# Zero matrix products among the first four tiles, setup work shared out over three engines, and a later test for the general path, in a biased-attention and channel-mix kernel

## The chip, the cores and the metric

The kernel runs on one core of one Trainium2 chip, as a single launch. The metric is the device time of that core in microseconds (us); lower is better. A core has a matrix engine (PE, with its weight loads PEld), a vector engine (DVE), a scalar engine (ACT), GpSimd (POOL) and a queue engine (SP) that here issues nearly all the transfers. Each engine works through its own list of instructions in a fixed order and waits on semaphores for the others.

## What is computed

The inputs are q, k, v of shape (4 batches, 8 heads, 768 positions, 64) and the weights of a channel mix with 512 model and 1024 hidden channels. Attention is causal within a window of n_local = 96 positions and sees n_global = 8 first positions as well, with a linear distance bias for each head; its output goes through the channel mix.

```python
scores = q @ k.T / 8 - slope[h] * dist          # dist = 96 for global keys outside the window
scores = where(is_global | is_local, scores, -1e9)
a = softmax(scores) ; x = a @ v                  # heads side by side: (4, 768, 512)
xk = mu_k * x + (1 - mu_k) * x_prev              # x_prev: one position earlier, zero at the start
xr = mu_r * x + (1 - mu_r) * x_prev
out = sigmoid(xr @ w_r) * (relu(xk @ w_k) ** 2 @ w_v)
```

The weights arrive as 64-bit floats and are split on the chip into a high and a low part, so that each product of the channel mix is three products on PE (high by high, high by low, low by high).

## The kernel before

**Tiling.** There are 24 tiles of 128 query positions, six to a batch. A loop over 25 steps runs `scores(step, hp)` for the tile of that step in four pairs of heads `hp`, `transposes(step - 1, hp)` for the tile before, and `weighted(step - 2, i)` for the one before that. Scores go to PSUM; DVE adds the bias pattern and takes the row maximum (L312), ACT takes the exponential (L313), DVE forms the reciprocal of the sum (L319, L320), DVE or POOL scales (L323), PE transposes (L335), ACT copies to SBUF (L337), and PE multiplies by v (L354). Two tiles make a chunk, and the channel mix of a chunk (`ffn`, L439) is cut into 40 pieces on PE that `run_ffn` threads between the attention steps from step 3 on; `mix` makes xk and xr (L378 to L383), `channel_mix` makes the products (L393 to L395), and L436 makes the output, which SP stores (L437).

**Weights.** The 20 blocks of 128 by 512 weights are loaded and split during the first steps: `weight_begin` issues the load from SP (L165) into a buffer that is shared with others, takes it through ACT (L172 for the eight blocks of w_k, L175 for the others), POOL (L173, w_k alone), DVE (L176 for the others, then L177, L178, L179) and ACT again (L180), and `weight_end` forms the low part on DVE (L186). `weights_go` after each head pair says how many blocks are to be begun and ended.

**The first microseconds.** SP loads the two sizes (L48) and the tiles of q, k and v. POOL makes the index ramps (L112 to L114) and then clears the upper halves of the two q buffers (L213) and of the three k buffers (L216), since the first eight tiles (`native`) multiply 128 rows of which 64 are zero. DVE turns the ramps and the sizes into distances (L115 to L125, L134 to L137). The bias pattern of a batch's first tile, `pat0`, has eight heads: six are made on DVE (L129), two on POOL (L131). The pattern of all other tiles, `pat`, is made half on ACT (L141) and half on POOL (L143). PE starts with ten products of a zero tile (L93), whose output `idle` nobody reads; they share three PSUM buffers (tag `f`) with the channel mix.

**The general path.** `wide()` handles sizes outside the fast path's limits. Seven small DVE instructions (L609 to L615) turn the sizes into a flag, every engine loads the flag into a register (L617) and branches on it (L618). With the given sizes the branch is not taken.

**What sets the order.** The program text gives each instruction a priority. A scheduler that replays the program on a simulated timeline then picks, for each engine, the ready instruction of highest priority, and that order is fixed in the program that runs. So an instruction need not run where it stands in the text: the flag's seven instructions are the last ones in the text, and the trace has them between 5.89 and 10.1 us. The tiles' buffers are given out by the same scheduler.

Of the kernel before, what the change touches and what calls it, by code (L numbers as in the profile page):

```python
# [9 lines left out]
F32 = mybir.dt.float32  # L10
F32R = mybir.dt.float32r
BF16 = mybir.dt.bfloat16
I32 = mybir.dt.int32
U32 = mybir.dt.uint32
AF = mybir.ActivationFunctionType
ALU = mybir.AluOpType
# [9 lines left out]
GMAX = 8  # L26
BACK = 96
LMAX = BACK + 1
# [11 lines left out]
def tile_biased_attention_channel_mix(ctx: ExitStack, tc: tile.TileContext, qT, kT, v, n_sizes, mu_kr, w_k, w_v, w_r, q_rows, k_rows, v_rows, slopes, out):  # L40
    nc = tc.nc
    vec, act, pool, pe = nc.vector, nc.scalar, nc.gpsimd, nc.tensor

    const = ctx.enter_context(tc.tile_pool(name="const", bufs=1))
# [6 lines left out]
    ngf, nlf = sizes[:, 0:1], sizes[:, 1:2]  # L51
# [34 lines left out]
    ps_f = fast.enter_context(tc.tile_pool(name="ps_f", bufs=3, space=PSUM))  # L86


    zeros = const.tile([128, 512], BF16, name="zeros")
    vec.memset(zeros, 0.0)  # L90
    for i in range(10):
        idle = ps_f.tile([128, 512], F32, name="idle", tag="f")
        pe.matmul(idle, zeros[:, 0:128], zeros, start=True, stop=True)  # L93

# [2 lines left out]
    pat0 = const.tile([128, H, 128], BF16, name="pat0")  # L99
# [4 lines left out]
    def piece():  # L104
        edge.append(next(cut))
        return btmp[:, edge[-2] : edge[-1]]

    ints, flts, local, glo, dist0, dist = (piece() for _ in range(6))
# [16 lines left out]
    vec.scalar_tensor_tensor(dist0, glo, nlf, local[:, 96:224], op0=ALU.max, op1=ALU.min)  # L125
    for h in range(H):
        c = -8.0 * 2.0 ** -(h + 1)
        if h < 6:
            vec.tensor_scalar(pat0[:, h, :], dist0, c, None, op0=ALU.mult)  # L129
        else:  # L130
            pool.tensor_scalar(pat0[:, h, :], dist0, c, 1.0, op0=ALU.mult, op1=ALU.mult)  # L131
# [6 lines left out]
    for h in range(H):  # L138
        c = -8.0 * 2.0 ** -(h + 1)
# [58 lines left out]
    def weights_need(n):  # L198
        weights_go(n, n)
# [5 lines left out]
    state = {}  # L205


    q_zero, k_ring = [], []
    for i in range(3):
        if i < 2:  # L210
            q_zero.append(q_pool.tile([128, H, 128], F32, name=f"qz_{i}", tag="qh"))
            kz = kw_pool.tile([128, H, W], F32, name=f"kz_{i}", tag="kw")[:, :, 0:128]
            pool.memset(q_zero[i][64:128], 0.0)  # L213
        else:
            kz = q_pool.tile([128, H, 128], F32, name=f"kz_{i}", tag="ql")
        pool.memset(kz[64:128], 0.0)  # L216
        k_ring.append(kz)
    k_first = const.tile([64, H, GMAX], F32, name="k_first")

    def first_keys(n):  # L220
        if n % NT:
            pool_copy(state[n - 1]["kr"][0:64, :, 128 - OWN : 128 - BACK], k_first)
        else:
            pool_copy(k_first, state[n]["kr"][0:64, :, 0:GMAX])
# [26 lines left out]
    def load_v(n):  # L251

        b, t = divmod(n, NT)
        va = v_pool.tile([128, DM], F32, name=f"va_{n}", tag="va")
        if t == 0:
            nc.sync.dma_start(va, v[b, 0:128, :])
            state[n]["va"] = [va]
            return
        vb = v_pool.tile([W - 128, DM], F32, name=f"vb_{n}", tag="vb")
        nc.sync.dma_start(va[0:GMAX], v[b, 0:GMAX, :])  # L260
        nc.sync.dma_start(va[GMAX:128], v[b, t * 128 - BACK : t * 128 + LATE, :])
        nc.sync.dma_start(vb, v[b, t * 128 + LATE : (t + 1) * 128, :])
        state[n]["va"] = [va, vb]
# [104 lines left out]
    def part(pool, tag, n):  # L368
        t = pool.tile([128, n * 256 + GAP.get(tag, 0)], F32R, name=tag, tag=tag)
        return t[:, 0 : n * 256].rearrange("p (a q) -> p a q", a=n)  # L370
# [15 lines left out]
    def channel_mix(xk, xr, out_rows, f_pool, f2_pool, ps_f):  # L386
        wkh, wkl = wts["k"]
        wrh, wrl = wts["r"]
        wvh, wvl = wts["v"]
        kkh, kkl = (part(f_pool, f"kk_{p}", 8) for p in ("hi", "lo"))  # L390

        def three(o, sh, sl, mh, ml, first, last):
            pe.matmul(o, sh, mh, start=first, stop=False)  # L393
            pe.matmul(o, sh, ml, start=False, stop=False)  # L394
            pe.matmul(o, sl, mh, start=False, stop=last)  # L395

        def z_of(i):
            z = ps_f.tile([128, 512], F32, name="z", tag="f")
            c = slice(i * 128, (i + 1) * 128)
            for k in range(4):  # L400
                three(z, xr[0][:, k, c], xr[1][:, k, c], wrh[:, k, :], wrl[:, k, :], k == 0, k == 3)
                yield
            sig = f2_pool.tile([128, 512], F32, name="sig", tag="f2")
            sigs.append((z, sig))

        sigs = []
        for fp in range(4):
            weights_need(4 if fp < 2 else 8)
            ps = ps_f.tile([128, 512], F32, name="kp", tag="f")
            for u in range(2):  # L410
                f = slice((2 * fp + u) * 128, (2 * fp + u + 1) * 128)
                o = ps[:, u * 256 : (u + 1) * 256]
                for k in range(4):
                    three(o, wkh[:, k, f], wkl[:, k, f], xk[0][:, k, :], xk[1][:, k, :], k == 0, k == 3)
                    if k % 2:
                        yield
            kk = f2_pool.tile([128, 2, 256], F32, name="kk", tag="f2")
            pv = ps.rearrange("p (a q) -> p a q", a=2)
            act.activation(kk, pv, AF.Relu)  # L419
            vec.tensor_mul(kk, pv, kk)  # L420
            act.copy(kkh[:, 2 * fp : 2 * fp + 2, :], kk)  # L421
            vec.tensor_sub(kkl[:, 2 * fp : 2 * fp + 2, :], kk, kkh[:, 2 * fp : 2 * fp + 2, :])  # L422
        weights_need(12)
        for i in range(2):
            yield from z_of(i)
        for z, sig in sigs:
            act.activation(sig, z, AF.Sigmoid)
        for i in range(2):
            c = slice(i * 128, (i + 1) * 128)
            vp = ps_f.tile([128, 512], F32, name="vps", tag="f")  # L430
            sig = sigs[i][1]
            for f in range(8):
                weights_need(13 + f)
                three(vp, kkh[:, f, c], kkl[:, f, c], wvh[:, f, :], wvl[:, f, :], f == 0, f == 7)
                yield
            vec.tensor_mul(sig, vp, sig)  # L436
            nc.sync.dma_start(out_rows(i), sig)  # L437

    def ffn(c):  # L439
# [2 lines left out]
        xr = mix(xt[:, :, 1:257], xt[:, :, 0:256], "r", p4k, f_pool, c == 0)  # L442
        return channel_mix(xk, xr, lambda i: out[(2 * c + i) * 128 : (2 * c + i + 1) * 128, :], f_pool, f2_pool, ps_f)


    LAG = 3
    queue = []
# [2 lines left out]
    def run_ffn(amount):  # L450
        budget[0] += amount
        while budget[0] >= 1.0 and queue:
            try:
                next(queue[0])
                budget[0] -= 1.0
            except StopIteration:
                queue.pop(0)
        if not queue:
            budget[0] = 0.0
# [3 lines left out]
    for step in range(NTILES + 1):  # L463
        if step + 1 < NTILES:
            load_tile(step + 1)
        if step == 0:
            load_v(0)
        if step < NATIVE:
            first_keys(step)
        for hp in range(4):  # L470
            if hp == 0 and step > 1:
                for i in range(4):
                    weighted(step - 2, i)
            if hp == 0 and 0 < step < NTILES:
                load_v(step)
            if step:
                transposes(step - 1, hp)
            if step < NTILES:
                scores(step, hp)
            if hp == 0:  # L480
                if step >= LAG and (step - LAG) % 2 == 0:
                    queue.append(ffn((step - LAG) // 2))
                    if len(queue) == 1 and step == LAG:
                        budget[0] = -17.5
            run_ffn(2.5)
            run_ffn(2.5)
            if hp == 1 and step + 1 < NTILES:
                split_tile(step + 1)
            slot = 4 * step + hp
            n = 2 + slot * 4 // 3 if slot < 7 else 8 + (slot - 6) * 6 // 7  # L490
            weights_go(n, n - 1 if n <= len(w_steps) else n)
# [112 lines left out]
                        pass  # L604


    okf = const.tile([128, 2], F32, name="okf")
    wide_i = const.tile([1, 1], I32, name="wide_i")
    vec.tensor_scalar(okf[:, 0:1], nlf, float(LMAX), None, op0=ALU.is_le)  # L609
    vec.tensor_scalar(okf[:, 1:2], nlf, 1.0, None, op0=ALU.is_ge)  # L610
    vec.tensor_mul(okf[:, 0:1], okf[:, 0:1], okf[:, 1:2])
    vec.tensor_scalar(okf[:, 1:2], ngf, float(GMAX), None, op0=ALU.is_le)
    vec.tensor_mul(okf[:, 0:1], okf[:, 0:1], okf[:, 1:2])
    vec.tensor_scalar(okf[:, 0:1], okf[:, 0:1], -1.0, 1.0, op0=ALU.mult, op1=ALU.add)
    vec.tensor_copy(wide_i, okf[0:1, 0:1])  # L615

    need_wide = nc.values_load(wide_i[0:1, 0:1], min_val=0, max_val=1)  # L617
    with tc.If(need_wide > 0):  # L618
        wide()
# [44 lines left out]
```

## Time and profile before

| | us |
|---|---|
| median of three runs (lowest, highest) | 517.16 (516.59, 517.49) |
| span of the profiled execution, first to last instruction | 515.0 |
| PE busy (with weight loads beside it: 436.7) | 493.2 |
| DVE busy | 356.2 |
| ACT busy | 329.5 |
| POOL busy | 217.0 |
| PE busy from 0 to 56 us | 41.0 |
| DVE busy from 0 to 56 us | 48.3 |

The profile gives the span of its execution, and no separate time for it; between the span and the median of the runs lie 2.2 us. A row of a view of stretches reads: from and to, length, then for PE, PEld, DVE, ACT and POOL the busy time and the number of instructions, then the granted share of the TensorE clock, the mean busy share of the sixteen DMA engines, and GB/s. A row of the timeline reads: start, length, engine, line, operation, output and inputs by name, shapes, count, and in brackets the idle time of the engine before it and what ended that. PE is nearly always busy from 56 us on.

### The profile page before, as it was taken

How to read it: one execution, taken by the hardware profiler on the slowest of the kernel's cores; microseconds unless marked ns; L12 is line 12 of the kernel's file. 1: busy time of each engine (PE TensorE's matmuls, PEld its weight loads, DVE VectorE, ACT ScalarE, POOL GpSimd, SP SyncE). 2: the span in 40 equal slices, each digit the busy share in tenths (PEclk: the TensorE clock that was granted, in tenths of full speed). 3: DMA queues.
4: the chain of work that ended last, by engine and by line, in shares of the span. 5: the costliest groups of instructions: out<-in, count | busy, mean ns of one | idle time of the engine just before them, and what ended most of it. 6: DMA issues, size and time to landing. Idle time of an engine off the chain costs nothing. (4 is left out here: it accounts for less than half of the span.)

```text
span 515.0 us, 10213 instructions
## 1 busy us (share of the span) xinstructions
PE 493.2 (96%) x3562; PEld 436.7 (85%) x3562; DVE 356.2 (69%) x896; ACT 329.5 (64%) x820; POOL 217.0 (42%) x363
## 2 busy tenths in 40 slices
PE   5876999999999999999999999999999999999995
PEld 3765998889898898898898898898898898898983
DVE  6899999977358767767777777767778765535321
ACT  4778679667537758757658667667668568554220
POOL 6333123453255556535547535536537535203000
PEclk7876899999999999999999999999999999999999
DMA  8995344415361441531522432432423211100101
GB/s 225 268 241 178 84 157 152 115 34 140 89 131 38 120 124 48 133 99 54 129 84 75 107 99 74 107 99 69 113 83 80 62 59 39 41 1 2 41 2 46
DMA packets 24714, 49.46 MB, mean 96 GB/s; under 512 B 5168, under 2 KB 9264, under 8 KB 24656
## 3 DMA queue, kind: packets, MB, share of 16 engines
q1 hardware_dynamic: 24512, 48.74, 34.9%
q8 instruction: 30, 0.49, 0.4%
q14 instruction: 28, 0.23, 0.1%
q10 hardware_dynamic: 144, 0.00, 0.0%
HBM read 42.44 MB, written 6.29 MB: 95 GB/s over the span
## 5 line engine op out<-in xcount | busy, mean ns | idle before, releaser
L323 POOL TENSOR_SCALAR e<-e,r 128x232 f32<-128x232 f32 (+1 forms) x168 | 81.8, 503 | 165.2 <-DVE r L320 141.9
L393 PE MATMUL kp<-xk_hi,wk_hi 128*128 128x256 f32 x384 | 109.0, 284 | 0.8 <-ACT xk_hi L382 0.8
L394 PE MATMUL kp<-xk_lo,wk_hi 128*128 128x256 f32 x384 | 107.5, 280 | 0.0
L395 PE MATMUL kp<-xk_hi,wk_lo 128*128 128x256 f32 x384 | 107.4, 280 | 0.0
L313 ACT ACTIVATE e<-e,nmax 128x232 f32<-128x232 f32 (+1 forms) x192 | 89.8, 471 | 23.1 <-DVE nmax L312 20.1
L312 DVE CUSTOM_DVE_ANT_0 e<-s,pat 128x232 f32<-128x232 f32 (+1 forms) x192 | 65.0, 373 | 22.7 <-PE s L307 14.1
L393 PE MATMUL vps<-wv_hi,kk_hi 128*128 128x512 f32 x192 | 75.3, 394 | 0.0
L395 PE MATMUL vps<-wv_hi,kk_lo 128*128 128x512 f32 x192 | 75.3, 392 | 0.0
L394 PE MATMUL vps<-wv_lo,kk_hi 128*128 128x512 f32 x192 | 75.2, 392 | 0.0
L393 PEld LDWEIGHTS kp<-xk_hi,wk_hi 128*128 128x128 f32 x384 | 72.3, 189 | 1.8 <-ACT xk_hi L382 1.1
L394 PEld LDWEIGHTS kp<-xk_lo,wk_hi 128*128 128x128 f32 x384 | 72.2, 188 | 0.6
L395 PEld LDWEIGHTS kp<-xk_hi,wk_lo 128*128 128x128 f32 x384 | 72.2, 188 | 0.0
L337 ACT COPY et<-t 128x256 f32<-128x256 f32 (+1 forms) x176 | 56.6, 373 | 18.2 <-PE t L335 17.5
L335 PE MATMUL t<-ident,e 128*128 128x128 f32 x352 | 57.8, 288 | 5.9 <-DVE e L323 5.9
L420 DVE TENSOR_TENSOR kk<-kp,kk 128x512 f32<-128x512 f32 x48 | 33.1, 689 | 42.7 <-ACT kk L419 42.5
L335 PEld LDWEIGHTS t<-ident,e 128*128 128x128 f32 x352 | 42.8, 142 | 14.9 <-DVE e L323 6.6
L422 DVE TENSOR_TENSOR kk_lo<-kk,kk_hi 128x512 fp32r<-128x512 f32 x48 | 34.5, 720 | 16.2 <-ACT kk_hi L421 15.8
L354 PE MATMUL av<-et,va 128*64 128x128 f32 x384 | 42.5, 290 | 2.7 <-ACT et L337 2.1
L421 ACT CAST kk_hi<-kk 128x512 fp32r<-128x512 f32 x48 | 29.9, 625 | 21.2 <-DVE kk L420 20.5
L419 ACT ACTIVATE kk<-kp 128x512 f32<-128x512 f32 x48 | 28.4, 591 | 23.2 <-PE kp L395 23.0
L395 PEld LDWEIGHTS vps<-wv_hi,kk_lo 128*128 128x128 f32 x192 | 36.0, 188 | 7.7
L394 PEld LDWEIGHTS vps<-wv_lo,kk_hi 128*128 128x128 f32 x192 | 36.2, 188 | 7.0 <-issue 0.2
(108 smaller groups left out, 1078.4 us busy)
## 6 DMA issues: line engine op xcount, KB each, us to landing
qraw<-in_qT_dram SPq DMA_DIRECT2D x32, 256.0 KB
kraw<-in_kT_dram SPq DMA_DIRECT2D x32, 256.0 KB
out_dram<-sig SPq DMA_DIRECT2D x24, 256.0 KB
va<-in_v_dram SPq DMA_DIRECT2D x20, 240.0 KB
vb<-in_v_dram SPq DMA_DIRECT2D x20, 208.0 KB
w<-in_w_k_dram SPq DMA_DIRECT2D x8, 512.0 KB
w<-in_w_v_dram SPq DMA_DIRECT2D x8, 512.0 KB
qz<-in_qT_dram SPq DMA_DIRECT2D x8, 256.0 KB
```

The source lines that it names most:

```text
L312: vec.tensor_tensor_reduce(out=e[:, :w], in0=o, in1=p[:, h, :], op0=ALU.add, op1=ALU.min, scale=-0.125, scalar=3.0e38, accum_out=s["nmax"] ...
L313: act.activation(e[:, :w], e[:, :w], AF.Exp, bias=s["nmax"][:, h : h + 1], scale=-1.0, accum_out=s["sum"][:, h : h + 1])
L323: (vec if n < 6 and u < 2 else pool).tensor_scalar(e[:, :w], e[:, :w], r[:, u : u + 1], 1.0, op0=ALU.mult, op1=ALU.mult)
L335: pe.transpose(pt[0:p, c : c + 128], e[:, k * 128 : k * 128 + p], ident)
L337: act.copy(et[0:p, k * 256 : k * 256 + 256], pt[0:p, k * 256 : k * 256 + 256])
L354: pe.matmul(o, vt[:, h * 64 : (h + 1) * 64], et[0:p, c + q : c + 128], start=k == 0, stop=k == nb - 1)
L393: pe.matmul(o, sh, mh, start=first, stop=False)
L394: pe.matmul(o, sh, ml, start=False, stop=False)
L395: pe.matmul(o, sl, mh, start=False, stop=last)
L420: vec.tensor_mul(kk, pv, kk)
L421: act.copy(kkh[:, 2 * fp : 2 * fp + 2, :], kk)
L422: vec.tensor_sub(kkl[:, 2 * fp : 2 * fp + 2, :], kk, kkh[:, 2 * fp : 2 * fp + 2, :])
```

## The change

- Twenty zero products stand at the front of the program where ten stood. Two more follow each head pair's scores in steps 0 to 3, 32 in all.
- The heads of `pat0` are shared out anew: the odd four on ACT, three of the even ones on DVE, one on POOL.
- The upper halves of the first q buffer and of the first k buffer are cleared on DVE, those of the other three on POOL as before.
- The seven instructions for the flag move into `find_path`, and must follow, on DVE, the multiplication of L436 that was traced last before step 8's scores of later heads.

```diff
     vec.memset(zeros, 0.0)
-    for i in range(10):
-        idle = ps_f.tile([128, 512], F32, name="idle", tag="f")
-        pe.matmul(idle, zeros[:, 0:128], zeros, start=True, stop=True)
+    def keep_warm(n):
+        for _ in range(n):
+            idle = ps_f.tile([128, 512], F32, name="idle", tag="f")
+            pe.matmul(idle, zeros[:, 0:128], zeros, start=True, stop=True)
+    keep_warm(20)
...
     for h in range(H):
         c = -8.0 * 2.0 ** -(h + 1)
-        if h < 6:
+        if h % 2:
+            act.mul(pat0[:, h, :], dist0, c)
+        elif h < 6:
             vec.tensor_scalar(pat0[:, h, :], dist0, c, None, op0=ALU.mult)
         else:
             pool.tensor_scalar(pat0[:, h, :], dist0, c, 1.0, op0=ALU.mult, op1=ALU.mult)
...
-            pool.memset(q_zero[i][64:128], 0.0)
+            (pool if i else vec).memset(q_zero[i][64:128], 0.0)
...
-        pool.memset(kz[64:128], 0.0)
+        (pool if i else vec).memset(kz[64:128], 0.0)
...
-            vec.tensor_mul(sig, vp, sig)
+            state["mul"] = vec.tensor_mul(sig, vp, sig)
...
+    okf = const.tile([128, 2], F32, name="okf")
+    wide_i = const.tile([1, 1], I32, name="wide_i")
+    def find_path(ins):
+        with tc.issue_after(ins.ins):
+            vec.tensor_scalar(okf[:, 0:1], nlf, float(LMAX), None, op0=ALU.is_le)
+            ...
+            vec.tensor_copy(wide_i, okf[0:1, 0:1])
...
             if hp == 0:
+                if step == 8:
+                    find_path(state["mul"])
                 if step >= LAG and (step - LAG) % 2 == 0:
                     queue.append(ffn((step - LAG) // 2))
...
+            if step < 4:
+                keep_warm(2)
             run_ffn(2.5)
             run_ffn(2.5)
...
-    vec.tensor_scalar(okf[:, 0:1], nlf, float(LMAX), None, op0=ALU.is_le)
...
-    vec.tensor_copy(wide_i, okf[0:1, 0:1])
     need_wide = nc.values_load(wide_i[0:1, 0:1], min_val=0, max_val=1)
```

More of the change, by code (lines that the diff above doesn't have):

```diff
@@ L443, in ffn @@
         return channel_mix(xk, xr, lambda i: out[(2 * c + i) * 128 : (2 * c + i + 1) * 128, :], f_pool, f2_pool, ps_f)
+    okf = const.tile([128, 2], F32, name="okf")
[3 more added lines that the diff above has]
+            vec.tensor_scalar(okf[:, 0:1], nlf, float(LMAX), None, op0=ALU.is_le)
+            vec.tensor_scalar(okf[:, 1:2], nlf, 1.0, None, op0=ALU.is_ge)
+            vec.tensor_mul(okf[:, 0:1], okf[:, 0:1], okf[:, 1:2])
+            vec.tensor_scalar(okf[:, 1:2], ngf, float(GMAX), None, op0=ALU.is_le)
+            vec.tensor_mul(okf[:, 0:1], okf[:, 0:1], okf[:, 1:2])
+            vec.tensor_scalar(okf[:, 0:1], okf[:, 0:1], -1.0, 1.0, op0=ALU.mult, op1=ALU.add)
+            vec.tensor_copy(wide_i, okf[0:1, 0:1])
     LAG = 3
@@ L604, in wide @@
                         pass
[L607 to L614, printed above, removed]
-    vec.tensor_copy(wide_i, okf[0:1, 0:1])
     need_wide = nc.values_load(wide_i[0:1, 0:1], min_val=0, max_val=1)
```

## The prediction

> **What bounds the kernel now.** I read the view of stretches first, cut where the busy shares change.
>
> ```profile
> 18.50:33.00 14.50, 10.44 (x84) 9.08 (x84) 14.34 (x47) 11.00 (x35) 3.83 (x6) 0.83 1.04 272
> ...
> 34.50:57.00 22.50, 17.21 (x112) 14.46 (x110) 22.50 (x59) 17.52 (x50) 6.50 (x10) 0.69 0.60 163
> ...
> 80.00:508.83 428.83, 428.58 (x3120) 381.97 (x3120) 283.21 (x660) 271.57 (x652) 189.09 (x307) 1.00 0.29 79
> ```
>
> And all of PE's waits after 56 us are this one:
>
> ```profile
> PE s L303 <- POOL kz L202: 0.4, 1, 0.4
> ```
>
> From 80 us on PE never rests (428.58 of 428.83). So the end comes a fixed amount of PE work after the place where PE becomes continuously busy, near 56 us. Before that DVE is the full engine: 14.34 of 14.50 and 22.50 of 22.50. PE's work there is partly at half clock, but PE mostly waits for DVE. What the change can gain is the time by which **DVE's stream before 57 us** moves forward.
>
> The clock changes on a raster of 3.41 us, so I cut the next view along it.
>
> ```profile
> 4.17:7.58 3.41, 1.45 (x11) 0.99 (x10) 3.35 (x18) 0.00 (x0) 3.13 (x7) 1.00 1.17 193
> ...
> 14.41:17.82 3.41, 3.41 (x19) 3.08 (x17) 1.62 (x8) 2.10 (x7) 1.74 (x4) 0.50 1.06 233
> ...
> 24.65:28.06 3.41, 1.25 (x10) 0.85 (x8) 3.41 (x11) 2.81 (x8) 1.19 (x3) 1.00 1.07 169
> ...
> 38.30:41.71 3.41, 1.31 (x10) 0.97 (x8) 3.41 (x9) 3.41 (x9) 2.49 (x5) 1.00 1.00 305
> ...
> 48.54:51.95 3.41, 2.61 (x11) 2.31 (x11) 3.41 (x10) 2.57 (x9) 0.66 (x1) 0.50 0.36 88
> 51.95:55.37 3.42, 3.20 (x15) 2.77 (x14) 3.42 (x10) 0.82 (x4) 0.00 (x0) 0.50 0.54 137
> ```
>
> After a window with PE busy 1.25 to 1.45 of 3.41 the clock falls to 0.50; it comes back only after one with 3.20 or more, and 2.61 does not do. Three dips follow, from 7.58 to 17.82, from 28.06, and from 41.71 to 55.37.
>
> The Trainium skill (TensorE: Matmul & The Clock Gate, "Why this matters for your kernels") warns only of PE gaps over some 3 us. By that rule nothing here needs warming. The windows above disagree: PE was busy 1.31 us in a window and lost the clock after it, so the measured shares decide.
>
> **Part by part. The first pattern.** The last two of POOL's memsets, then DVE's own timeline:
>
> ```profile
> 4.62 2.07 POOL L216 MEMSET kz<- 64x1024 f32 x2
> ```
>
> ```profile
> 0.87 0.27 DVE L90 MEMSET zeros<- 128x256 uint32 x1 [0.87 <-PEq L654]
> ...
> 4.11 0.59 DVE L55 CAST words<-sizes_w 128x4 f32<-128x4 int32 x1 [2.11 <-DMA sizes_w<-in_n_sizes_dram]
> ...
> 5.72 1.03 DVE L134 TENSOR_SCALAR btmp<-btmp,sizes 128x96 f32<-128x96 f32 x1
> 5.89 0.86 DVE L609 TENSOR_SCALAR okf<-sizes 128x1 f32<-128x1 f32 x1
> ...
> 6.02 0.74 DVE L124 TENSOR_TENSOR btmp<-btmp 128x128 f32<-128x128 f32 x1
> ...
> 7.57 1.31 DVE L129 TENSOR_SCALAR pat<-btmp 128x128 bf16<-128x128 f32 x6
> ...
> 9.06 0.28 DVE L312 CUSTOM_DVE_ANT_0 e<-s,pat 128x128 f32<-128x128 f32 x1
> ```
>
> L134, L609 and L124 start at different times, all end at 6.75 to 6.76, just behind POOL's memsets (4.62 + 2.07 = 6.69). They were held; a free L124 of 128 elements costs some 0.2. With two of POOL's five memsets gone, POOL ends two memsets, 2.07, earlier, and the hold of about 0.75 goes. By the Trainium skill (SBUF — State Buffer, "Who interferes with whom") a DVE operation that uses both ports and a GpSimd operation shut each other out for a whole instruction. The common end at 6.76 agrees; the rule changes no term.
>
> Three of six L129 leave: 3 x 1.31 / 6 = 0.65. Of the flag's seven operations, those ahead of L312 cost DVE about 0.4 in issue steps (estimate from the starts, 5.89 to 6.02 for the first two, and 8.80 to 9.06 before L312). The two memsets come to DVE: 1024 elements each where L90 clears 256 in 0.27, so about 1.1 each, 2.2 in all, in the 2.11 that DVE waits for the sizes; uncovered they would cost those 2.2, covered 0.1. Sum on DVE: 0.75 + 0.65 + 0.4 - 0.1 = 1.7, L312 at about 7.4. But ACT takes four products more:
>
> ```profile
> 7.62 1.26 ACT L141 ACTIVATE pat<-btmp 128x232 bf16<-128x232 f32 x4 [5.17 <-DVE btmp L135]
> 9.38 0.40 ACT L313 ACTIVATE e<-e,nmax 128x128 f32<-128x128 f32 x1 [0.51 <-DVE nmax L312]
> ```
>
> At no more than 1.26 for four, and starting about 1 us earlier, ACT is free near 9.0 instead of 8.88, so the first exponential comes at 9.0 instead of 9.38. Of DVE's 1.7, ACT lets through 0.4; POOL loses one of two L131, nothing behind it is urgent.
>
> **The zero products.** Ten cost PE this now, and a product of 512 columns at full clock steps as in the tail:
>
> ```profile
> 1.20 3.57 PE L93 MATMUL idle<-zeros 128*128 128x512 bf16 x9 [1.20 <-DVE zeros L90]
> 6.72 1.26 PE L304 MATMUL s<-kz,qz 128*128 128x128 f32 x8 [1.96 <-POOL kz L216]
> ...
> 497.68 0.39 PE L393 MATMUL vps<-wv_hi,kk_hi 128*128 128x512 f32 x1
> 497.91 0.39 PE L394 MATMUL vps<-wv_lo,kk_hi 128*128 128x512 f32 x1
> ```
>
> 9 in 3.57 is 0.40 each, mostly cold; 497.91 - 497.68 = 0.23 warm. Forty-two more cost 9.7 to 16.8 us of PE. Between 8.4 and 55.4 PE has 47.0 - 35.33 = 11.67 idle, and half-clock work that would shrink.
>
> ```profile
> 8.40:55.40 47.00, 35.33 (x219) 30.56 (x218) 42.82 (x145) 36.38 (x110) 15.81 (x29) 0.68 0.85 236
> ```
>
> Nothing but the zero tile and a PSUM buffer holds a zero product back, and the scheduler moves ready work forward (L609 stands last in the text and ran at 5.89). So I expect the 42 to fill PE's first gaps, mainly up to 20 us, not to stay spread over four tiles. Ten at the front fill 4.77 to about 7.1, at a cost of up to 0.4 on the first scores (6.72), which L312 cannot use before 7.4. The first dip goes; the second and third stay.
>
> What the first dip costs DVE is seen in its waits:
>
> ```profile
> 10.87 0.29 DVE L312 CUSTOM_DVE_ANT_0 e<-s,pat 128x128 f32<-128x128 f32 x1 [0.77 <-PE s L304]
> ...
> 11.84 0.29 DVE L312 CUSTOM_DVE_ANT_0 e<-s,pat 128x128 f32<-128x128 f32 x1 [0.45 <-PE s L304]
> ...
> 15.67 0.40 DVE L312 CUSTOM_DVE_ANT_0 e<-s,pat 128x232 f32<-128x232 f32 x1 [1.44 <-POOL wa L173]
> ...
> 17.27 0.40 DVE L312 CUSTOM_DVE_ANT_0 e<-s,pat 128x232 f32<-128x232 f32 x1 [0.53 <-PE s L304]
> ```
>
> 0.77 + 0.45 + 1.44 + 0.53 = 3.2 us, scores at half clock (the third names POOL; I count it too, since this L312 reads tile 1's first scores). At full clock I take 2.4 of it, three quarters, since ACT's exponentials still pace it. With ACT's 0.4 DVE would reach 18.5 us about 2.8 earlier; bounds 0.4 (no clock gained) and 1.7 + 3.2 = 4.9.
>
> **What is late next.** The transfers are: a stretch up to 33.6 us, and one late block of w_k from SP through ACT and POOL to DVE.
>
> ```profile
> 3.00:33.60 30.60, 22.05 (x135) 17.77 (x134) 25.94 (x108) 19.72 (x65) 13.68 (x27) 0.74 1.05 276
> ```
>
> ```profile
> 24.31 2.38 SPq L165 DMA_DIRECT2D w<-in_w_k_dram  x3
> ```
>
> ```profile
> 32.94 0.68 ACT L172 ACTIVATE wa<-w 128x512 f32<-128x512 f32 x1 [1.50 <-DMA w<-in_w_k_dram]
> 33.52 0.61 ACT L180 CAST wk_hi<-w 128x512 fp32r<-128x512 f32 x1
> ```
>
> ```profile
> 34.12 0.61 POOL L173 TENSOR_SCALAR wa<-wa 128x512 f32<-128x512 f32 x1
> ```
>
> ```profile
> 35.53 1.18 DVE L177 TENSOR_SCALAR wa<-wa 128x512 int32<-128x512 int32 x2
> ```
>
> The DMA engines' share is 1.05 from 3.0 to 33.6: always backlogged. The block issued at 24.31 reached ACT at 32.94, over 8 us later. Issued earlier it waits longer in the same backlog. ACT's next instruction starts at 33.52, and POOL's 0.61 behind that puts L177 at 34.15 at the earliest, where it ran at 35.53: DVE's gain there is capped at **1.4**. Behind it DVE is full to 57 us, so 1.4 is what arrives. The half-clock stretch ahead of 56 us adds little: PE's products of the channel mix need xk_lo from DVE.
>
> ```profile
> 55.16 1.22 DVE L383 TENSOR_TENSOR xk_lo<-mix_k,xk_hi 128x1024 fp32r<-128x1024 f32 x1
> 56.98 0.39 PE L394 MATMUL kp<-xk_lo,wk_hi 128*128 128x256 f32 x1
> ```
>
> L383 ends at 56.38, PE starts at 56.98, so a warm PE would gain at most 0.6 there; I count none, the zero products being spent by then.
>
> **The flag.** Behind L436 in mid-program its seven operations, a microsecond or so together (estimate, twice their 0.4 of issue steps above), fall where DVE is busy 283 of 429; a register load on SP may wait a microsecond ahead of loads with steps to spare. Cost 0; at most 1, if a step's loads had no slack. The tail keeps its form.
>
> **Sum.** Of the span 515.0, 1.4 goes: 513.6. The median of runs stands 517.16 - 515.0 = 2.16 above the span, so **515.7**; this case reaches from 515.0 (1.4 + 0.6) to 516.6.
>
> **Rivals.**
> - *The DMA cap does not hold*: the order of DVE or of the loads shifts, and DVE does other work while the block is on its way. Then up to 2.8 to 4.9 arrive: 512.3 to 514.4, likeliest 513.5. For it: L177 has neighbours that do not need the block. Against: queues are strict and shares were 1.05.
> - *Nothing arrives*: the exponentials of tile 0 keep their pace behind ACT's four products, or the new order gives the 1.4 back in the full DVE stretch: 517.2, 516.2 to 518.0.
> - *The zero products stand in the way (slower)*: they outrank scores of tiles 1 to 3 and run at half clock, 2 x 0.40 ahead of each of tile 1's four pairs, 3.2 us on a path where DVE already waits for PE; less 1.2 for the shorter front and the cap's reserve, DVE arrives 2.0 late: 519.2. It decides where more of them stand between PE's scores than its gaps hold, 11.67 of gaps against 16.8 cold; warm, 9.7 fit. That the clock is not held at all is the same case with fewer of them in the way.
>
> **How the numbers follow.** The forecast 0.42, cap void 0.20, nothing 0.18, slower 0.20. A measurement here tells about 0.2%, 1.03 us, from no change. Faster: 0.42 x 0.85 + 0.20 + 0.18 x 0.1 = 0.58; same 0.20; slower 0.22. The range takes in most of both outer cases: 512.6 to 519.0. The forecast's own range is 515.0 to 516.6.
>
> **What would show it.** Right: L312 first near 7.4 to 7.9 and the first exponential near 9.0; granted clock 1.00 from 4 to 18 us; most zero products before 20 us; DVE with a hole before the L177 that waits for the late w_k block, ACT's wait for it still near 33; L394's first product near 55.5. Wrong: that block landing before 32, or L394 before 54 (cap void); zero products between tile 1's scores and DVE waiting longer for PE (slower); a clock of 0.50 at 8 to 17 us all the same.

## The result, and the profile after

| | before | after |
|---|---|---|
| median of runs, us (lowest, highest) | 517.16 (516.59, 519.28) | 521.13 (519.57, 521.63) |
| span of the profiled execution, us | 515.0 | 518.8 |
| time of that execution, us | not given | 520.66 |

The changed kernel is slower: the ratio of the times is 1.0069, with a 95% interval of 1.0055 to 1.0083. The prediction was 515.7, in a range of 512.6 to 519.0.

The view of stretches of the changed kernel, in the columns explained ahead (length, PE, PEld, DVE, ACT, POOL, clock, DMA share, GB/s):

```profile
8.40:18.50 10.10, 10.10 (x68) 7.67 (x67) 6.72 (x33) 8.29 (x32) 3.51 (x8) 1.00 1.04 328
18.50:33.00 14.50, 11.09 (x78) 7.05 (x77) 13.84 (x46) 9.05 (x25) 3.14 (x7) 1.00 1.05 262
34.50:57.00 22.50, 17.27 (x94) 14.71 (x94) 21.01 (x54) 17.47 (x49) 6.79 (x10) 0.58 0.46 141
...
80.00:512.00 432.00, 432.00 (x3151) 384.72 (x3150) 287.29 (x676) 274.20 (x663) 187.05 (x310) 1.00 0.29 80
```

From 80 us on PE is busy all the time, as before, so the loss arose earlier. The granted clock was 1.00 through the first 33 us, as was meant; whether the added zero products did that is taken up with e8 below. But DVE, which was full from 18.5 to 33 and from 34.5 to 57 before (14.34 and 22.50), now has holes there: 0.66 and 1.49.

All 52 zero products ran early, between 1.2 and 29.9 us (a row of the view of one tile: shortest, median and longest duration in ns, then first and last start), and the front, the work up to some 20 us, came forward. Rows of DVE, ACT and PE from the timeline:

```profile
L95 PE MATMUL idle<-zeros x52: 379/379/635, 1.2 to 29.9; 128*128 128x512 bf16 x52
```

```profile
5.71 0.27 DVE L140 TENSOR_SCALAR btmp<-btmp,sizes 128x96 f32<-128x96 f32 x1
...
8.03 0.29 DVE L318 CUSTOM_DVE_ANT_0 e<-s,pat 128x128 f32<-128x128 f32 x1 [0.59 <-PE s L310]
...
11.54 0.29 DVE L318 CUSTOM_DVE_ANT_0 e<-s,pat 128x128 f32<-128x128 f32 x1 [2.15 <-PE s L310]
```

```profile
8.73 0.38 ACT L319 ACTIVATE e<-e,nmax 128x128 f32<-128x128 f32 x1
```

```profile
8.63 2.42 PE L95 MATMUL idle<-zeros 128*128 128x512 bf16 x8
10.89 0.61 PE L310 MATMUL s<-kz,qz 128*128 128x128 f32 x4
...
18.34 0.41 PE L310 MATMUL s<-kz,qz 128*128 128x128 f32 x2
```

(L140, L310, L318 and L319 are L134, L304, L312 and L313 of before; most lines moved by 6.) L140 takes 0.27 us where it took 1.03, so POOL no longer holds DVE. The first reduction starts at 8.03 instead of 9.06, the first exponential at 8.73 instead of 9.38. Eight zero products stand ahead of tile 0's second half of scores, for which DVE waits 2.15 us; even so tile 1's last scores start at 18.34. In the kernel before they started at 19.88:

```profile
19.88 0.41 PE L304 MATMUL s<-kz,qz 128*128 128x128 f32 x2
```

The front is 1.5 us early.

That is gone 15 us later. The same place on ACT in both kernels, before first: tile 1's first transposes are copied to SBUF (L337, now L343), and PE's attention products of tile 1 wait for them.

```profile
28.74 0.68 ACT L175 ACTIVATE wa<-w 128x512 f32<-128x512 f32 x1 [1.28 <-DMA w<-in_w_r_dram]
29.32 1.18 ACT L337 COPY et<-t 128x256 f32<-128x256 f32 x4
```

```profile
31.93 0.66 ACT L178 ACTIVATE w<-w 128x512 f32<-128x512 f32 x1 [1.86 <-DMA w<-in_w_k_dram]
32.50 0.63 ACT L343 COPY et<-t 128x256 f32<-128x256 f32 x2
33.32 0.68 ACT L178 ACTIVATE wa<-w 128x512 f32<-128x512 f32 x1 [0.19 <-DMA w<-in_w_k_dram]
33.91 0.63 ACT L343 COPY et<-t 128x256 f32<-128x256 f32 x2
```

And PE, before first:

```profile
31.74 0.76 PE L303 MATMUL s<-kz,qz 128*128 128x104 f32 x2
```

```profile
32.91 0.43 PE L360 MATMUL av<-et,va 128*64 128x128 f32 x2 [2.66 <-ACT et L343]
...
35.56 0.76 PE L309 MATMUL s<-kz,qz 128*128 128x104 f32 x2
...
60.44 0.39 PE L400 MATMUL kp<-xk_lo,wk_hi 128*128 128x256 f32 x1
```

Before, all four copies ran ahead of the steps of the late w_k blocks. Now two stand behind the first late block's step and two behind the second's. PE stands idle for 2.66 us, tile 2's last pair of scores starts at 35.56 instead of 31.74, and the first product with xk_lo at 60.44 instead of 56.98: 3.46 of the 3.8 us by which the span grew. The Trainium skill (PSUM — Partial Sum Buffer, "Engine vs sequencer instructions") says that ACT's, DVE's and POOL's queues are strictly first in, first out; these rows agree, since the copy waits behind a step that it has nothing to do with.

The chain that ended last (start, us, what) tells it in order:

```profile
22.74 10.50 DMA w<-in_w_k_dram
33.32 0.68 ACT wa L178
34.01 0.27 ACT et L343
34.32 1.32 PE av L360 x8
```

The loads were put into another order too. SP's queue, changed kernel first, then before: tile 2's q (qz) now stands behind one block of w_k and one of w_r.

```profile
10.13 0.36 SPq L171 DMA_DIRECT2D w<-in_w_k_dram  x1
11.26 0.35 SPq L171 DMA_DIRECT2D w<-in_w_r_dram  x1
12.59 0.48 SPq L246 DMA_DIRECT2D qz<-in_qT_dram  x1
```

```profile
11.72 0.48 SPq L240 DMA_DIRECT2D qz<-in_qT_dram  x1
...
12.96 0.36 SPq L165 DMA_DIRECT2D w<-in_w_k_dram  x1
```

Nothing in the diff touches these copies or loads. The scheduler fixes each engine's order from its own replay of the program, and with the edit, all of it outside these copies and loads, it chose another one.

### The profile page after: what moved, and what is told of

Same layout as the page of the kernel before. It is cut to its first block, busy times and chain, and to the rows that moved or that the text cites. A ratio compares the mean times of both kernels' runs of the same rounds, so it can differ in the third digit from the quotient of the medians.

```text
span 518.8 us, 10292 instructions
## 1 busy us (share of the span) xinstructions
PE 500.9 (97%) x3604; PEld 439.6 (85%) x3604; DVE 359.2 (69%) x895; ACT 330.5 (64%) x824; POOL 216.3 (42%) x360
## 4 chain that ended last, share of the span: by engine, by line
PE 91%; DVE 3%; DMA 3%; ACT 2%; POOL 0%; issue 0%; DVEq 0%; ACTq 0%; POOLq 0%
PE kp L399 9%; PE kp L400 9%; PE kp L401 9%; PE vps L399 9%; PE vps L401 9%; PE vps L400 8%; PE av L360 8%; PE t L341 7%; PE z L399 4%; PE z L401 4%; PE z L400 4%; PE s L313 3%; PE s L312 3%; PE s L310 3%; DMA w<-in_w_k_dram 2%; PE s L309 2%
## 5 line engine op out<-in xcount | busy, mean ns | idle before, releaser
L329 POOL TENSOR_SCALAR e<-e,r 128x232 f32<-128x232 f32 (+1 forms) x168 | 84.2, 518 | 153.4 <-DVE r L326 122.3
L401 PE MATMUL kp<-xk_hi,wk_lo 128*128 128x256 f32 x384 | 107.4, 280 | 0.0
L319 ACT ACTIVATE e<-e,nmax 128x232 f32<-128x232 f32 (+1 forms) x192 | 89.6, 470 | 24.5 <-DVE nmax L318 23.9
L318 DVE CUSTOM_DVE_ANT_0 e<-s,pat 128x232 f32<-128x232 f32 (+1 forms) x192 | 64.5, 372 | 26.9 <-PE s L313 14.6
L401 PE MATMUL vps<-wv_hi,kk_lo 128*128 128x512 f32 x192 | 75.3, 392 | 0.0
L401 PEld LDWEIGHTS kp<-xk_hi,wk_lo 128*128 128x128 f32 x384 | 72.1, 188 | 0.2
L343 ACT COPY et<-t 128x256 f32<-128x256 f32 (+1 forms) x176 | 56.5, 372 | 15.8 <-PE t L341 15.4
L341 PE MATMUL t<-ident,e 128*128 128x128 f32 x352 | 55.1, 280 | 2.0 <-DVE e L329 2.0
L341 PEld LDWEIGHTS t<-ident,e 128*128 128x128 f32 x352 | 41.2, 137 | 10.8 <-issue 2.5
L427 ACT CAST kk_hi<-kk 128x512 fp32r<-128x512 f32 x48 | 29.9, 624 | 22.1 <-DVE kk L426 19.9
L401 PEld LDWEIGHTS vps<-wv_hi,kk_lo 128*128 128x128 f32 x192 | 36.0, 188 | 7.8
```

The lines of the kernel that those rows point to most:

```text
L318: vec.tensor_tensor_reduce(out=e[:, :w], in0=o, in1=p[:, h, :], op0=ALU.add, op1=ALU.min, scale=-0.125, scalar=3.0e38, accum_out=s["nmax"] ...
L319: act.activation(e[:, :w], e[:, :w], AF.Exp, bias=s["nmax"][:, h : h + 1], scale=-1.0, accum_out=s["sum"][:, h : h + 1])
L329: (vec if n < 6 and u < 2 else pool).tensor_scalar(e[:, :w], e[:, :w], r[:, u : u + 1], 1.0, op0=ALU.mult, op1=ALU.mult)
L341: pe.transpose(pt[0:p, c : c + 128], e[:, k * 128 : k * 128 + p], ident)
L343: act.copy(et[0:p, k * 256 : k * 256 + 256], pt[0:p, k * 256 : k * 256 + 256])
```

## The experiments: first the zero products and one pair of copies

Theory A was that the loss is in that order; theory B, the prediction's own slower rival, that zero products stand in PE's way. Four kernels were made. A dependency that carries no semaphore (NoSync) puts one instruction ahead of another in the scheduler's order and does nothing else.

**e1_copies_first**: the changed kernel, with the four copies of tile 1's first two head pairs ahead of the steps of the late blocks 5 and 6.

```diff
-            act.activation(a.bitcast(F32), top.bitcast(F32), AF.Abs, scale=2.0**111)
+            w_act[i] = act.activation(a.bitcast(F32), top.bitcast(F32), AF.Abs, scale=2.0**111)
...
+            c = act.copy(et[0:p, k * 256 : k * 256 + 256], pt[0:p, k * 256 : k * 256 + 256])
+            if n == 1 and hp in (0, 1):
+                for i in (5, 6):
+                    tc.add_manual_dep(w_act[i].ins, c.ins.name, mybir.DependencyInfo(mybir.DependencyClass.NoSync, mybir.DependencyReason.DATA), reason="order")
```

> The changed kernel with one thing more: on ACT the first four copies of tile 1's transposed e (L343) are made to stand ahead of the steps that take in w_k blocks 5 and 6 (L178); the first 38 ACT instructions are as in the changed kernel. Theory A (order on ACT): in the changed kernel these copies ran at 32.5 and 33.9 behind blocks that landed late, and PE's product with v, the last scores of tile 2 and all behind them waited; so the copies come near 30, the last scores of tile 2 near 32 instead of 35.6, and the time falls by 2.5 to 4 us, to 517 to 518.5. Theory B (the zero products stand in PE's way): the 52 products are all still there, the time stays within 1 us of 521.1.

Measured: 518.68 us, ratio 1.0026 [1.0005, 1.0046]. All zero products are still there, and the copies run early:

```profile
30.51 1.17 ACT L344 COPY et<-t 128x256 f32<-128x256 f32 x4
...
32.91 0.69 ACT L179 ACTIVATE w<-w 128x512 f32<-128x512 f32 x1 [1.23 <-DMA w<-in_w_k_dram]
```

Some 2.4 of the 4.0 us come back with every part of the change in place. The scheduler moved other work on ACT and PE as well, so this is the worth of the copies and the plan made around them together. A's range ended a little too low.

**e2_blocks_first**: the kernel before, with the same copies pushed behind blocks 5 and 6.

```diff
+            if (n, hp) in {(1, 0): (5,), (1, 1): (6,)}:
+                for i in {(1, 0): (5,), (1, 1): (6,)}[n, hp]:
+                    tc.add_manual_dep(c.ins, w_act[i].ins.name, mybir.DependencyInfo(mybir.DependencyClass.NoSync, mybir.DependencyReason.DATA), reason="order")
```

> The kernel before, with the opposite order forced on ACT: the copies of tile 1's first two head pairs (L337) stand behind the steps that take in w_k blocks 5 and 6 (L172). No zero product is added. Theory A: the blocks land near 33 to 34, the copies move from 29.3 to 33.5 or later, and the time rises by 3 to 5 us, to 520 to 522. Theory B: no change, 516.5 to 518.

Measured: 518.83, ratio 1.0036 [1.0023, 1.0048]: the sign that A expects, half its size. The copies ran at 35.60, as meant; the plan around them is a new one too, and what in it gives the other half back was not tested.

**e3_ten_zero**: the changed kernel with ten zero products in front and none in the steps.

```diff
-    keep_warm(20)
+    keep_warm(10)
...
-            if step < 4:
-                keep_warm(2)
```

> The changed kernel with ten zero products at the front, as before, and none in the steps. In its order on ACT the first copies of tile 1 stand ahead of the late w_k blocks. Theory A: 515.5 to 518, since the order is good again. Theory B: the zero products are gone, so the time also falls, to 515 to 517; this run alone does not tell the two apart, e4 is its counterpart.

Measured: 521.90, ratio 1.0085 [1.0068, 1.0103]. Both theories missed it. A loss of this size needs none of the 42 extra products; as the plan is new, it is not shown to be the same loss. Again copies stand behind a late block, other copies this time (ACT, then PE):

```profile
38.43 0.67 ACT L178 ACTIVATE wa<-w 128x512 f32<-128x512 f32 x1 [2.52 <-DMA w<-in_w_k_dram]
39.01 1.17 ACT L343 COPY et<-t 128x256 f32<-128x256 f32 x4
```

```profile
39.42 0.75 PE L360 MATMUL av<-et,va 128*64 128x128 f32 x3 [4.97 <-ACT et L343]
```

PE's longest wait of this kind, 7.38 us up to 53.33, ends in the same way, with copies behind the step of a w_v block.

**e4_zero_alone**: the kernel before with all the zero products and nothing else of the change (`keep_warm` as in the diff).

> The kernel before with the zero products of the change alone (20 at the front, 2 after each head pair of steps 0 to 3). In its order on ACT the first copies of tile 1 stand ahead of the late w_k blocks. Theory A: 515.5 to 518, all 52 zero products notwithstanding. Theory B: 519.5 to 522, as the zero products stand in PE's way here too.

Measured: 518.51, ratio 1.0024 [1.0006, 1.0043], between the two theories' ranges: about a third of the loss, the part and its new plan together, although the granted clock was 0.92 in the stretch from 34.5 to 57 us (before: 0.69).

## The experiments: parts and order taken apart

Any edit makes a new plan, so single edits cannot tell a part's cost from that of the plan. The next four kernels hold the order fixed. Each score product, transpose, attention product, reduction, exponential, copy, scaling, weight step and load is kept by name, and the order in which the kernel before has them on its five queues, up to some 75 us, is written in as chains of NoSync dependencies. Only the zero products, the first pattern, the memsets, the flag and the channel mix are left to the scheduler.

```diff
+PINNED = {'ACT': [('ex', 0, 0), ('ex', 0, 1), ('ex', 0, 2),
...
+            K["wa", i] = act.activation(a.bitcast(F32), top.bitcast(F32), AF.Abs, scale=2.0**111)
...
+            K["et", n, hp, k] = act.copy(et[0:p, k * 256 : k * 256 + 256], pt[0:p, k * 256 : k * 256 + 256])
...
+    for chain in PINNED.values():
+        for x, y in zip(chain, chain[1:]):
+            tc.add_manual_dep(K[y].ins, K[x].ins.name, mybir.DependencyInfo(mybir.DependencyClass.NoSync, mybir.DependencyReason.DATA), reason="order")
```

**e5_old_order**: all parts of the change, order of before.

> The changed kernel, all of its parts in it, with the order in which the kernel before has its score products, transposes, attention products, exponentials, copies, weight steps and loads on PE, ACT, DVE, POOL and SP up to some 75 us written into it; only the zero products, the first pattern, the memsets, the flag and the channel mix are placed by the scheduler. Theory A (the loss is in the new order of the queues, the parts themselves gain at the front): 514.5 to 516.5, about my forecast of 515.7, ratio 0.995 to 0.999. Rival B (zero products stand in PE's way wherever they are): 518 to 520. Rival C (pattern, memsets or flag cost by themselves): 519 to 521.

**e6_old_order_ten**: the same with ten zero products (e3's edit).

> The changed kernel with only the ten zero products at the front and none in the steps, with the same written order of the kernel before. Theory A: 515.5 to 517.0 (the front's gain without the held clock; order alone took the 521.9 of the run without the extra products away). Rival B: 515 to 516.5, and faster than the run with all zero products by 1 us or more. Rival C: 519 to 521.

**e7_new_order**: the program of before, with the changed kernel's order in the chains.

> The kernel before, none of the change's parts in it, with the order that the changed kernel has on PE, ACT, DVE, POOL and SP up to some 75 us written into it. Theory A (order): 519.5 to 522, ratio 1.004 to 1.009, with the copies of the transposes behind late w_k blocks on ACT. Rivals B and C (the parts): 516.5 to 517.8.

**e8_flag_alone**: the program of before with `find_path` alone; the scheduler kept its order but for one q load.

> The kernel before with the flag alone moved behind the sixth channel-mix product and its register load with it; the order of the queues is that of before but for tile 2's q load, one place earlier on SP. Theory A: 516.3 to 517.4, no change that can be told. Rival C, the flag's part: 518 or more, from a late register load holding up loads on SP or from DVE in mid-program.

| us, median | order of before | order of after |
|---|---|---|
| program of before | 517.23 | **521.26** (e7), ratio 1.0074 [1.0057, 1.0091] |
| program of after | **517.27** (e5), ratio 1.0013 [0.9991, 1.0035] | 521.13 |
| program of after, ten zero products | **517.04** (e6), ratio 0.9991 [0.9979, 1.0004] | |

The order is the loss. The changed kernel's order costs 4.0 us with none of the change's parts in the program, and with the old order no cost or gain of all the parts together can be told: e5's interval reaches from -0.5 to +1.8 us, e6's from -1.1 to +0.2. In e7 the copies stand where the changed kernel has them (ACT):

```profile
32.00 0.63 ACT L412 COPY et<-t 128x256 f32<-128x256 f32 x2
...
33.92 0.63 ACT L412 COPY et<-t 128x256 f32<-128x256 f32 x2
```

Tile 2's last scores start at 35.58 there and the first product with xk_lo at 60.47, within 0.03 us of the changed kernel. e8 gave 516.73, ratio 0.9999 [0.9985, 1.0013]: no cost of the flag can be told.

e8's trace shows one thing more. It has ten zero products and the old setup, and yet (before, then e8):

```profile
0.00:18.50 18.50, 12.81 (x54) 8.80 (x55) 11.68 (x62) 9.41 (x30) 12.21 (x31) 0.72 0.91 234
```

```profile
0.00:18.50 18.50, 14.49 (x82) 9.96 (x83) 13.81 (x63) 11.35 (x39) 12.56 (x32) 1.00 0.92 226
```

The clock was 1.00 here, and tile 1's last scores started at 16.84, earlier than in the changed kernel. From 8.4 to 18.5 us e2 and e3, with ten zero products, show 1.00 too, where the kernel before shows 0.53. So it is not shown that the added zero products keep the first dip away, nor how much of the front's 1.5 us comes from the change. From 18.5 to 33 us the changed kernel and e1, e4, e5, e9 and e12 show 1.00 and e13 0.88, all with 52; of the kernels with ten, e14 shows 1.00 and the others 0.75 to 0.88. And e8's early front brought nothing: that execution took 518.52 us.

So theory A held for the loss, but its forecast of a gain in e5 and e6 did not (517.04 lies just outside its range). Why the 1.4 did not arrive there, from e5 (weight steps L254, cast L262, low part L268 in its numbering; ACT, then DVE, then DVE of the kernel before):

```profile
33.34 0.67 ACT L254 ACTIVATE wa<-w 128x512 f32<-128x512 f32 x1 [1.83 <-DMA w<-in_w_k_dram]
33.92 0.60 ACT L262 CAST wk_hi<-w 128x512 fp32r<-128x512 f32 x1
```

```profile
32.48 0.20 DVE L401 TENSOR_SCALAR r<-sum 128x4 f32<-128x4 f32 x1
...
34.55 0.70 DVE L268 TENSOR_TENSOR wk_lo<-w,wk_hi 128x512 fp32r<-128x512 f32 x1 [1.56 <-ACT wk_hi L262]
```

```profile
33.44 0.16 DVE L319 TENSOR_SCALAR r<-sum 128x4 f32<-128x4 f32 x1
...
34.61 0.69 DVE L186 TENSOR_TENSOR wk_lo<-w,wk_hi 128x512 fp32r<-128x512 f32 x1
```

DVE comes to this stretch 1.0 us early (L401 is L319 of before). Then it needs the cast of block 0, and the cast stands on ACT right behind the step that waits for the late block 6. It starts its low part at 34.55; in the kernel before this was 34.61. Of the 1.0 us, 0.06 is left.

## The experiments: an order that lets the front's gain through

In the next three the written order of before is changed in one stretch: on ACT the first four copies of tile 1's transposes go ahead of the step of block 10, and the cast of block 0, the other four copies and tile 2's last exponentials ahead of the steps of blocks 6, 5 and 7; on DVE four steps of blocks 8, 9 and 10 and tile 3's first two reductions go ahead of the first step of block 6.

```diff
-  ('wa', 10), ('et', 1, 0, 0), ('et', 1, 0, 1), ('et', 1, 1, 0), ('et', 1, 1, 1), ('ex', 2, 2), ('ex', 2, 3), ('wa', 6), ('hi', 0),
+  ('et', 1, 0, 0), ('et', 1, 0, 1), ('et', 1, 1, 0), ('et', 1, 1, 1), ('ex', 2, 2), ('ex', 2, 3), ('wa', 10), ('hi', 0),
...
```

**e9_freed_order**: the changed kernel in this order.

> The changed kernel, all parts in it, with the written order of the kernel before but for one stretch: on ACT the cast of w_k block 0 and the copies of tile 1's transposes go ahead of the weight steps that wait for late loads (blocks 10, 6, 5, 7), and on DVE the steps of blocks 0, 8, 9 and 10 go ahead of the first step of block 6. Theory A, sharper (what stands in the queues behind the late block set the end in the run with the old order, DVE came there 1.0 us early and waited 1.56 us for that cast): the wait goes and the front's gain arrives, 514.5 to 516.3. Rival D (the gain cannot arrive in any order, DVE's stream after the late block is full and starts when the block is there): 516.7 to 517.6.

**e10_freed_ten**: the changed kernel with ten zero products in this order.

> The same order, with only the ten zero products at the front. Theory A: 514 to 516.3, as fast as the run with all of them or faster by up to 0.5 us, since PE has no zero products between scores. Rival B, what is left of it: 0.7 us or more faster than the run with all of them. Rival D: 516.7 to 517.6.

**e11_freed_before**: the program of before in this order.

> The kernel before, none of the change's parts, with the same freed order. Theory A: DVE comes to the stretch 1 to 2 us later than in the changed kernel, so this one gains little, 516.0 to 517.2, slower than the changed kernel in the same order by 0.5 to 2 us. Rival E (the order alone brings all, the parts of the change nothing): the same time as the two runs above within 0.4 us.

Measured: e10 515.99, ratio 0.9978 [0.9960, 0.9995], faster than both kernels of this study, by 0.05 to 0.4% of the kernel before; e9 518.73, 1.0022 [1.0007, 1.0037]; e11 519.01, 1.0026 [1.0007, 1.0044]. For e10 theory A held. DVE has no hole left up to 33 us, where e6 in the old order had 1.55 (e6, then e10):

```profile
18.50:33.00 14.50, 7.55 (x61) 6.36 (x58) 12.95 (x41) 9.52 (x29) 3.37 (x6) 0.75 1.05 273
```

```profile
18.50:33.00 14.50, 11.65 (x82) 10.42 (x78) 14.50 (x48) 12.11 (x38) 3.97 (x7) 0.76 1.06 273
```

For e9 and e11 it did not hold, and neither did rivals D and E: both were slower than before. Their front is late in the profiled executions (520.04 and 518.60 us). Tile 1's last scores start at 17.58 in e10, but at 20.44 in e9, where ten zero products run ahead of them, and at 20.16 in e11, without the shared setup work and with a clock of 0.50 from 9 to 18 us (e10, then e9):

```profile
17.58 0.41 PE L386 MATMUL s<-kz,qz 128*128 128x128 f32 x2
```

```profile
12.27 2.32 PE L170 MATMUL idle<-zeros 128*128 128x512 bf16 x10
...
20.44 0.41 PE L386 MATMUL s<-kz,qz 128*128 128x128 f32 x2
```

Why a late front costs more in this order than in the old one is not shown: ACT's waits for the transposes ahead of tile 1's copies are short in all three, 0.7 us in e9, 0.8 in e11 and 1.5 in e10. But B has a place after all: in this order the extra zero products cost 518.73 - 515.99 = 2.7 us. And the setup parts with the flag, which are worth nothing in the old order, are worth 519.01 - 515.99 = 3.0 us here, as medians; how much of it goes by the setup work itself is open, since e11's trace also has the slower clock. The single times of e9 and e11 spread over 516.6 to 520.3, where all but one of e10's lie between 515.7 and 516.4; what decides within that spread was not tried.

## The experiments: which queue

Three more went after what was open: which single queue carries the loss, and what comes after the late blocks.

**e12_loads_only**: the changed kernel and its own written order, but SP's chain from the kernel before.

> The changed kernel with its own order written in on PE, ACT, DVE and POOL, and only the loads on SP in the order of the kernel before (tile 2's q ahead of w_k block 0 and w_r block 8, block 6 ahead of block 5). Theory A1 (the loss sits on ACT): no gain or a small one, 520 to 521.6. Rival F (the loss sits in the loads, tile 2's q comes 1.5 us late): 517 to 519.

Measured: 539.92, ratio 1.0453 [1.0437, 1.0470], far outside both theories. Tile 2's q came early, as meant. But SP now loads block 6 ahead of block 5 while ACT takes 5 first, and issues the load of block 11 only at 46.07, when ACT has been waiting for it since 44.39:

```profile
34.82 0.66 ACT L253 ACTIVATE w<-w 128x512 f32<-128x512 f32 x1 [4.23 <-DMA w<-in_w_k_dram]
...
50.57 0.66 ACT L256 ACTIVATE wa<-w 128x512 f32<-128x512 f32 x1 [6.18 <-DMA w<-in_w_r_dram]
```

**e13_act_only**: the changed kernel and its own written order on all queues, with only ACT's first steps of blocks 5, 6 and 7 moved, behind the copies, the cast and four exponentials.

> The changed kernel with its own order written in on all queues but for three instructions on ACT: the first steps of w_k blocks 5, 6 and 7, which wait for their loads, go behind the copies of tile 1's first two transposes, the cast of block 0 and the exponentials of tile 2's heads 2 to 5. Theory A1: most of the loss goes, 517.5 to 519.2. Rival F: 520 to 521.6.

Measured: 522.02, ratio 1.0094 [1.0079, 1.0109]. No gain; theory A1 missed, and rival F by 0.4. Tile 2's scores did end 3 us earlier, but DVE's chain wants block 5 where it stood, and POOL makes tile 3's k buffer ready behind the same blocks' steps (DVE, then PE):

```profile
36.37 0.43 DVE L258 TENSOR_SCALAR w<-w 128x512 int32<-128x512 int32 x1 [3.77 <-POOL w L254]
```

```profile
39.53 0.76 PE L384 MATMUL s<-kz,qz 128*128 128x104 f32 x2 [5.08 <-POOL kz L283]
```

The stop went from ACT to DVE and POOL. Neither the old order on SP alone nor these three steps on ACT alone gave the loss back; DVE, POOL and PE were not tried alone. In both tries the queues no longer fitted one another.

**e14_freed_more**: e10 with DVE's remaining waits for blocks 6, 5 and 7 filled by other work.

> The changed kernel with ten zero products in the freed order, and 2.8 us of DVE's waits for blocks 6, 5 and 7 filled: the steps of blocks 8, 9 and 10, tile 2's scaling and tile 3's reductions go between them on DVE, tile 3's exponentials and the casts of blocks 8 to 10 on ACT, tile 2's scaling on POOL. If the late blocks were the cap and DVE's waits for them are filled: 513.5 to 515.6, 0.4 to 2.4 us faster than the freed order. If what follows (blocks 4 and 11, landing later still) is the next cap: 515.7 to 516.5, no gain on the freed order.

Measured: 518.92, ratio 1.0036 [1.0022, 1.0051], outside both ranges. DVE's waits for 6, 5 and 7 went, but the next ones on ACT are for blocks that land later, the cast of xk_hi stands behind the last of them, and PE waits 7.62 us for it (ACT, then PE):

```profile
51.08 0.67 ACT L256 ACTIVATE wa<-w 128x512 f32<-128x512 f32 x1 [1.93 <-DMA w<-in_w_v_dram]
51.66 1.03 ACT L463 CAST xk_hi<-mix_k 128x1024 fp32r<-128x1024 f32 x1
```

```profile
52.74 0.80 PE L474 MATMUL kp<-xk_hi,wk_hi 128*128 128x256 f32 x2 [7.62 <-ACT xk_hi L463]
```

In every plan traced here ACT waits for loads of weights; what the best plan would give stays open.

## Why the prediction was wrong

- **The end follows PE's start near 57 us: right.** That start moved by 3.46 us and the span by 3.8.
- **The first pattern, memsets and flag: right in kind.** POOL's hold of DVE is gone (L140), the first exponential came at 8.73 (forecast 9.0). L318 ran at 8.03 rather than 7.4 to 7.9, as it had to wait for scores. No cost of the flag can be told (e8).
- **The zero products float to the front: right in the main.** 33 of the 52 started before 20 us. They did not fill PE's gap ahead of the first scores: nine ran there, as before, and PE stood idle from 5.22 to 6.80. The clock stayed at 1.00 to 33 us, but that they hold it is not shown (e8). That DVE's waits for PE's scores would shrink by 2.4 was wrong: up to 18.5 us they were 3.6 us, where the text counted 3.2 before, and the longest, 2.15 at 11.54, is a new one behind eight zero products.
- **The front's lead at 18.5 us: 1.5 us on PE, forecast 2.8 on DVE** in bounds of 0.4 to 4.9. In e5, with the order of before, DVE's reduction that ran at 19.43 before ran at 17.82, 1.6 early. Right sign, about half the size.
- **"The cap", the step that failed for the gain.** The text took one late block through ACT, POOL and DVE's L177, found room for 1.4 and wrote that 1.4 is what arrives. It asked what the block itself releases, not what else stands behind its step on ACT. With the old order that is the cast of block 0, and the room is 0.06, not 1.4 (e5).
- **The queues' order taken as given, the step that failed for the time.** All its rows are of the old order, and the sum moves instructions within it; a new order is a term that it puts at nothing. The change made a new order, and that order alone costs 4.0 us (e7). The text even used that the scheduler moves ready work, for the zero products, but not for the copies and loads. Which move in the new order costs how much stays open: the copies are the one that the chain shows, and moving them back returned 2.4 (e1).
- **Rivals.** The slower one had the right sign and, with 519.2, was short by 1.9. Its sign appeared, zero products between tile 1's scores and longer waits for PE, but its mechanism was not the cause: the new order costs the same with ten zero products (e7), and the old order with all 52 costs nothing that can be told (e5). "Nothing arrives" (517.2) is what happened when the order was held (517.27 and 517.04), though by another cause than the two that it names. That the order shifts was in two rivals, as a gain where the cap is void and as a loss of no more than the 1.4 where nothing arrives; a loss beyond that was in none.
- **Two sums are a little off, without weight:** 1.4 + 0.6 off the kernel before gives 515.2, not 515.0, and 33.52 + 0.61 is 34.13, not 34.15.

## What to carry to other kernels

Where a scheduler writes the order, a small edit at the front is two changes: its own cost and a new plan for everything behind it. Compare the two programs' orders queue by queue before reading times, and price a part only with the order held. For each step that waits for a late load, list what stands behind it on its queue and who waits for that. An order can pay with one set of parts and cost with another, so parts and order have to be tried together (e10 against e9 and e11).

## What the runs showed of the hardware

- Zero products that come with a held clock can be worth nothing. From 0 to 18.5 and from 18.5 to 33 us the clock was 1.00 in e5; in e6, with 42 fewer, it was 0.91 and 0.75. e5 took 517.27 us, e6 517.04.
- The clock of the same first microseconds differs between traces with ten zero products: 0.53 from 8.4 to 18.5 us in the kernel before, 1.00 in e2, e3 and e8. What decides it was not tested.
- The changed kernel's instructions with another order of loads took 539.92 us instead of 521.13 (e12): SP brought the blocks in one order and ACT took them in another, and all that stood behind ACT's head waited with it.
